# Eight table evacuations split by filter group, with a new order of the LN1 statistics and of the filter stages, in a one-core spectral block and gated FFN

## The chip, the cores and the metric

The kernel runs on one core of a Trainium2 chip. The metric is device time in microseconds (us) of one execution, as the median of several. All runs compared here are fast runs at full granted clock, except that three executions in two experiments (named below) show 0.997. A profile of one execution stands beside the times; its "span" runs from the first to the last instruction that it shows and is about 2 us shorter than the time. Engines: PE is the matmul engine, PEld its weight loads, DVE the vector, ACT the scalar engine, POOL the GpSimd. PSUM is the memory that the matmuls write, here used as eight banks; to evacuate a bank is to copy it into SBUF, the working memory, so that the bank can be written again.

## The reference, cut to what matters

```python
def _A_ref(x, w_r, w_i):                       # x: (1, 2048, 576)
    X = jnp.fft.rfft2(x.astype(jnp.float32), axes=(-2, -1))
    X = X * (w_r + 1j * w_i)
    return jnp.fft.irfft2(X, s=(S, D), axes=(-2, -1)).astype(jnp.bfloat16)
def _B_ref(x, w_gate, w_up, w_down):           # 576 -> 4608 -> 576
    return (_gelu(x @ w_gate) * (x @ w_up)) @ w_down
h  = x + _A_ref(_layernorm(x), A_w_r, A_w_i)
h2 = h + _B_ref(_layernorm(h), B_w_gate, B_w_up, B_w_down)
```

## The kernel before

The Fourier transforms are matmuls with constant tables, in this order:

- **Head.** x arrives in five transfers as 16 tiles. LN1, the first layer norm, takes each tile's variance, on DVE (`B`: two statistics instructions) or on ACT (`S` and `Q`: a sum and a sum of squares). Six groups of tiles follow: DVE aggregates (`v`), ACT takes the root (`q`), DVE the reciprocal (`c`), DVE or POOL scales the table (`x`), POOL negates half of x (`n`), PE multiplies (`M`), and five PSUM banks a group are evacuated to the tile `U` (`E0` to `E29`; `A` is ACT, `D` is DVE).
- **Filter stage.** For each of 16 frequency groups: `D` (six matmuls on U, evacuation CUS), `B` (four, evacuation YS), `T` and `Z` (products and sums with the spectral weights on DVE), `V` (four matmuls, evacuation), and five times `R` (two matmuls and an expansion VR on DVE).
- **Inverse, LN2, FFN.** Not changed.

An order of work is a list of words; each engine takes its own words in order, and the semaphores follow from the buffers named in `r` (read) and `w` (written).

```python
def a_bank(i, k):                    # the PSUM bank of evacuation (group i, part k)
    return (5 * i + AORD.index(k) + ABASE) % 8
def a_ev(n, eng):                    # one evacuation of the table stage
    ...
    dst = U[0:w, k, :, c0:c1, :].rearrange("p g n e -> p n g e")
    P.op(eng, fn, r=[("PS", b)], w=[("U", i, k)])
def st_D(i, eng=ACT):
    g = GORD[i]                      # 1 .. 15, 0
    ...   # each matmul reads all of U's part k
          r=uk[us] + ["FT"], w=[("PS", b)])
def st_T(i, ...):                    # DVE product of YS with the weights
    ...
```

Of the kernel before, what the change touches and what calls it, by code (L numbers as in the profile page):

```python
# [9 lines left out]
S, D, K2 = 2048, 576, 289  # L10
KW = 288
HK = 144
# [4 lines left out]
NG = 16  # L17
# [3 lines left out]
NPRE = 8  # L21
PARTS = ((0, 256), (256, 512))
GROUPS = ((0, 2), (2, 4), (4, 7), (7, 10), (10, 13), (13, 16))
SEQ1 = """k14 B0 B1 v0 Q2 S2 B3 q0 v1 n0 n2 c0 q1 S4 x0D c1 M0 E1A B6 E0A Q4 B5 B7 x1P v2 E2D n1 B8 E3A E4A k104 M1 q2 c2 B9 Q10 E5A E7A n3 v3 S10 B12 E6A q3 c3 x2P B11 k202 M2 E9A x3P Q13 v4 E12A E8A q4 n4 B14 c4 B15 E10A E11A S13 E13D M3 E14A E15A v5 x4P E16D q5 E17A c5 E18A M4 n5 x5D E20D E19A E22D E21A M5 E23D E24A E25A E27A E26D E29A E28D""".split()
LORD = "x0-2 x2-4 a0-4 x4-8 a4-8 x8-12 x12-16 a8-16".split()
ACT_TILES = tuple(int(w[1:]) for w in SEQ1 if w[0] == "Q")
SEQF = """w0 w1 D0 D1 D2 B0 T0 B1 T1 Z0 D3 B2 D4 B3 D5 T2 Z1 B4 Z2 D6 T3 T4 V0 D7 B5 Z3 B6 w2 Z4 R0 T5 V1 D8 Z5 B7 T6 Z6 D9 B8 T7 V2 D10 V3 Z7 T8 Z8 D11 B9 R1 V5 B10 w3 T10 T9 D12 Z10 V4 D13 B11 Z9 T11 V6 B12 Z11 B13 T12 D14 T13 V8 Z13 D15 V7 Z12 B14 R2 B15 T14 V10 T15b V9 Z14 V11 V13 T15a Z15a V12 V14 Z15b R3 V15 R4""".split()
VENG = [('act',), ('act',), ('act',), ('act',), ('act',), ('act',), ('act',), ('act',), ('act',), ('act',), ('act',), ('act',), ('act',), ('act',), ('act',), ('act', 'act')]
DENG, BENG = ['act', 'dve', 'dve', 'act', 'act', 'act', 'act', 'act', 'act', 'act', 'act', 'act', 'act', 'act', 'act', 'act'], ['dve', 'act', 'act', 'act', 'act', 'act', 'act', 'act', 'act', 'act', 'act', 'act', 'act', 'act', 'act', 'act']
QR = ((0, 2), (2, 3), (3, 4), (4, 8), (8, 16))  # L30
DSTEP, DLAG = (36, 22) if NPRE == 8 else (28, 22)
SEQ = """I0 I1 N0 I2 s0 N1 I3 s1 N2 I4 q0 s2 c0 N3 I5 s3 p1 q1 N4 q2 I6 N5 c1 c2 p0 A1 I7 n3 N6 A0 z3 N7 p2 D2 G0 G1""".split()
# [11 lines left out]
def build_tables():  # L44
# [8 lines left out]
    n1 = np.arange(128)[:, None]  # L53
    n2 = np.arange(16)[None, :]
    s = 16 * n1 + n2
    A = np.zeros((128, 16, 64, 2))
    I = np.zeros((64, 2, 16, 128))
    for j in range(64):
        if j == 0:
            A[:, :, 0, 0] = 1.0  # L60
            A[:, :, 0, 1] = (1 - 2 * (n1 % 2))
            I[0, 0] = 1.0
            I[0, 1] = (1 - 2 * (np.arange(128) % 2))[None, :]
        else:
            th = 2 * np.pi * ((j * s) % 2048) / 2048.0
            A[:, :, j, 0] = np.cos(th)
            A[:, :, j, 1] = -np.sin(th)
            I[j, 0] = np.cos(th).T
            I[j, 1] = -np.sin(th).T
    A = A.reshape(128, 16, 4, 16, 2).transpose(0, 1, 3, 2, 4)  # L70
    I = I.reshape(4, 16, 2, 16, 128).transpose(1, 0, 2, 3, 4)
    T["ATAB"] = A.reshape(128, 16 * 128)
    I = I.reshape(128, 16, 128)
# [19 lines left out]
    B = np.zeros((2, 3, 16, 4, 2, 128))  # L93
    V = np.zeros((2, 2, 128, 2, 16, 4, 2))
    nn = np.arange(16)
    for st in range(2):
        g = 1 - st
        for p in range(128):
            half, r, jj = p // 64, (p % 64) // 4, p % 4
            low = (g + 16 * jj) if half == 0 else _minus_rows(g)[jj]  # L100
            k = 128 * r + low
            w = np.exp(-2j * np.pi * ((k * nn) % 2048) / 2048.0)
            if low in (0, 64):
# [3 lines left out]
                c = np.conj(w)  # L107
# [5 lines left out]
            if half == 0:  # L113
                sl = jj
                e = np.exp(-2j * np.pi * ((r * nn) % 16) / 16.0)
                ca, cb = e, 1j * e
            else:
                sl = (128 - low - g) // 16
                rp = 15 - r
                e = np.exp(-2j * np.pi * ((rp * nn) % 16) / 16.0)  # L120
# [190 lines left out]
def _build(nc, A_x, A_w_r, A_w_i, B_w_gate, B_w_up, B_w_down, out):  # L311
    P = Prog(nc)
    T = build_tables()
    dram = {n: nc.inline_tensor(_np_bf16(T[n]), name="c_" + n.lower()) for n in T}
    PE, DVE, ACT, SP, POOL = "pe", "dve", "act", "sp", "pool"
# [50 lines left out]
    U = sb.alloc("U", [128, 5, NG, NT, 8], BF16)  # L366
# [7 lines left out]
    FT = sb.alloc("FT", [128, 6, 2 * HK], BF16)  # L374
# [26 lines left out]
    PS = nc.alloc_psum_tensor("PS", [128, 4096], F32)  # L401

    def bank(b, p0=0, p1=128, c0=0, c1=512):
        return PS[p0:p1, b * 512 + c0:b * 512 + c1]

    def banks(b, n, w):
        return PS[:, b * 512:(b + n) * 512].rearrange("p (a c) -> p a c", a=n)[:, :, 0:w]
# [17 lines left out]

    for i, w in enumerate(LORD):
        (x_load if w[0] == "x" else atb_load)(i, int(w[1:].split("-")[0]), int(w.split("-")[1]))
# [25 lines left out]
    GORD = list(range(1, NG)) + [0]  # L453
# [23 lines left out]
    def ln1_var(i):  # L477
        c0, c1 = GROUPS[i]
        for c in range(c0, c1):
            if c in ACT_TILES:  # L480
                P.op(DVE, lambda v, c=c: v.tensor_scalar(TM[:, 0, c:c + 1], SA[:, 0, c:c + 1], SA[:, 0, c:c + 1], 1.0 / (D * D), op0=ALU.mult, op1=ALU.mult), r=[("SA0", c)], w=[("TM", c)])
            else:
                P.op(DVE, lambda v, c=c: v.bn_aggr(MV1[:, c, :], ST1[:, c, :, :]), r=[("ST1", c, 0), ("ST1", c, 1)], w=[("MV1", c)])
        for c in range(c0, c1):
            if c in ACT_TILES:
                P.op(DVE, lambda v, c=c: v.tensor_scalar(MV1[:, c, 1:2], SA[:, 1, c:c + 1], 1.0 / D, TM[:, 0, c:c + 1], op0=ALU.mult, op1=ALU.subtract), r=[("SA1", c), ("TM", c)], w=[("MV1", c)])
# [23 lines left out]
    def a_bank(i, k):  # L510
        return (5 * i + AORD.index(k) + ABASE) % 8
# [19 lines left out]
                    P.op(PE, lambda t, b=b, lhs=lhs, p0=p0, p1=p1, s=s, e=e, o=o, c=c: t.matmul(bank(b, p0, p1, o, o + 128), lhs, ATS[:, c, :], start=s, stop=e),  # L531
                         r=[("X", c), ("ATS", c)] + ([("XN", c)] if k % 2 else []), w=[("PS", b)])

    def a_ev(n, eng):
        i, k = n // 5, AORD[n % 5]
        c0, c1 = GROUPS[i]
        n, b, w = c1 - c0, a_bank(i, k), 64 if k == 4 else 128
        src = bank(b, 0, w, 0, 128 * n).rearrange("p (n g e) -> p n g e", n=n, g=16)
        dst = U[0:w, k, :, c0:c1, :].rearrange("p g n e -> p n g e")
        fn = (lambda v: v.tensor_copy(dst, src)) if eng == DVE else (lambda a: a.activation(dst, src, ACTF.Copy))  # L540
        P.op(eng, fn, r=[("PS", b)], w=[("U", i, k)])

    def x_neg(i):
        c0, c1 = GROUPS[i]
# [1 line left out]
             r=[("X", c) for c in range(c0, c1)], w=[("XN", c) for c in range(c0, c1)])  # L546

    ENG = {"A": ACT, "D": DVE, "P": POOL}
    RUN1 = {"k": idle_mm, "S": act_sum, "Q": act_sq, "B": ln1_tile, "v": ln1_var, "q": ln1_sqrt, "c": ln1_rs, "M": a_mm, "x": ln1_scale, "E": a_ev, "n": x_neg}
    P.op(ACT, lambda a: a.activation(SA[:, 0, 0:1], EPT[:, 0:1], ACTF.Sqrt), r=["EPT"], w=[("SA0", 0)])  # L550
    for w in SEQ1:
        a = w[1:]
        RUN1[w[0]](*((int(a[:-1]), ENG[a[-1]]) if a[-1] in ENG else (int(a),)))


    c = 0
    while c < NT:
        c1 = c + 1
        while c not in ACT_TILES and c1 < NT and c1 not in ACT_TILES:
            c1 += 1  # L560
        src, f, keys = (SA[:, 0, c:c1], -1.0 / D, "SA0") if c in ACT_TILES else (MV1[:, c:c1, 0], -1.0, "MV1")
        P.op(POOL, lambda g, c=c, c1=c1, src=src, f=f: g.tensor_scalar(NM[:, c:c1], src, f, 1.0, op0=ALU.mult, op1=ALU.mult),
             r=[(keys, k) for k in range(c, c1)], w=[("NM", k) for k in range(c, c1)])
        c = c1
    P.alias([("XN", c) for c in range(NT)], [("V", g, c) for g in range(NG) for c in range(2)])
    uk = [[("U", i, k) for i in range(len(GROUPS))] + (["Uz"] if k == 4 else []) for k in range(5)]
    ukeys = [k for ks in uk for k in ks]
    LAST = NG - 1

    FB, used = {}, [0] * 8  # L570
    for t, w in enumerate(SEQF):
        k, i = w[0], w[1:].rstrip("abc")
        if k in "DB":
            late = ("V", 0) in FB or any(x[0] == "V" for x in SEQF[t:t + 4])
            b = min((0, 2, 4) if late else (0, 2, 4, 6), key=lambda b: max(used[b], used[b + 1]))
            used[b] = used[b + 1] = t + 1
        elif k in "VR":
            b = min((6, 7) if ("D", LAST) not in FB else range(8), key=lambda b: used[b])
            used[b] = t + 1
            if k == "V":  # L580
# [4 lines left out]
                b = (b, b2)  # L585
# [4 lines left out]
    def ev(eng, dst, src, r, w):  # L590
        fn = (lambda v: v.tensor_copy(dst, src)) if eng == DVE else (lambda a: a.activation(dst, src, ACTF.Copy))  # L591
        P.op(eng, fn, r=r, w=w)

    def st_D(i, eng=ACT):
        g = GORD[i]
        b0, s3 = FB["D", i], i % 3
        for o in range(2):
            b = b0 + o
            for m, us in enumerate((1 - o, 3 - o, 4) if o == 0 else (4, 1 - o, 3 - o)):
                P.op(PE, lambda t, b=b, m=m, us=us, o=o, g=g: t.matmul(bank(b, 0, 128, 0, 2 * HK), U[:, us, g, :, :], FT[:, 3 * o + (2 if us == 4 else us // 2), :], start=(m == 0), stop=(m == 2)),  # L600
                    r=uk[us] + ["FT"], w=[("PS", b)])
        ev(eng, CUS[:, s3, :, :].rearrange("p a (j r) -> p a j r", r=2), banks(b0, 2, 2 * HK).rearrange("p r (a j) -> p a j r", a=2),
           [("PS", b0), ("PS", b0 + 1)], [("CU", s3)])

# [59 lines left out]

    for w in SEQF:
        i = int(w[1:].rstrip("abc"))
# [42 lines left out]
    g0 = smm.index("G0")  # L709
    for t, w in enumerate(w for w in smm if w[0] != "G"):  # L710
        b = min((2, 3) if t >= g0 - 2 else range(4), key=lambda b: last[b])
# [251 lines left out]
def bass_sequential_preLN__spectral_gfnet__geglu_ffn__prompt_kernel(  # L963
    nc, A_x, A_w_r, A_w_i, B_x, B_w_gate, B_w_up, B_w_down, out
):
    _build(nc, A_x, A_w_r, A_w_i, B_w_gate, B_w_up, B_w_down, out)
# [28 lines left out]
```

## Time and profile before

| | before |
|---|---|
| median time | 492.23 us (3 runs, 492.04 to 492.62) |
| span of the profiled run | 490.0 us |
| PE busy | 484.2 us (99%) |
| x tiles 4 to 6 in hand (POOL starts on them) | 7.63 us |
| first d-transform matmul, D0 | 19.58 us |
| first B matmul, B0 | 21.95 us |
| first matmul of the inverse | 48.30 us |

PE is the critical engine, so the reader should look for the few places where it waits; those that the profile lists all lie before the inverse or at its start. The lines are in the prediction. The start times are those of the first instruction as the profile lists it; the chain of waits puts B0 at 22.12, 0.17 later, as it counts from the end of the matmul ahead.

### The profile page before, as it was taken

Reading aid. Unit: us, or ns where it says so; the run is one execution under the profiler, and the core shown is the slowest. Engines: PE = TensorE matmul, PEld = TensorE weight load, DVE = VectorE, ACT = ScalarE, POOL = GpSimd, SP = SyncE. Lnnn points to the kernel's source line nnn. Section 1 sums busy time; section 2 is a strip of 40 time slices with the busy share of each in tenths; the row PEclk is TensorE's granted clock in tenths of the full one; section 3 lists DMA queues with packets and bytes.
Section 4 is the critical chain, followed back from the end, with each engine's and each line's share of the span. In section 5 each row is a group of like instructions: output and inputs, shape, how many; then the busy total and the mean of one; then the engine's idle time right before and its main releaser. Section 6 shows DMA issues by size and latency. Waiting matters only on the chain.

```text
span 490.0 us, 9898 instructions
## 1 busy us (share of the span) xinstructions
PE 484.2 (99%) x4373; PEld 285.7 (58%) x4374; DVE 190.9 (39%) x381; ACT 150.9 (31%) x291; POOL 33.4 (7%) x61
## 2 busy tenths in 40 slices
PE   7999999999999999999999999999999999999998
PEld 3787754444588744444577644444677544444775
DVE  6999623443455534333311144433211233333111
ACT  6899852233222222322200033233100122323000
POOL 6411541000000020000000000000000000000000
PEclk9999999999999999999999999999999999999999
DMA  8990997211000071100000001000000000000000
GB/s 281 242 324 18 373 372 272 70 25 21 1 14 17 13 233 23 23 4 1 1 18 14 19 18 23 17 0 1 7 19 19 7 0 1 1 1 1 14 19 18
DMA packets 25147, 31.26 MB, mean 64 GB/s; under 512 B 11440, under 2 KB 17840, under 8 KB 25104
## 3 DMA queue, kind: packets, MB, share of 16 engines
q1 hardware_dynamic: 22208, 18.68, 13.1%
q0 software_dynamic: 2896, 11.95, 6.9%
q8 instruction: 34, 0.56, 0.5%
q14 instruction: 9, 0.07, 0.1%
HBM read 26.29 MB, written 2.36 MB: 58 GB/s over the span
## 4 chain that ended last, share of the span: by engine, by line
PE 96%; DVE 1%; DMA 1%; SPq 0%; POOL 0%; issue 0%; POOLq 0%; DVEq 0%
PE PS L839 57%; PE PS L926 29%; PE PS L600 2%; PE PS L610 2%; PE PS L531 1%; PE PS L717 1%; DMA XO<-in_A_x_dram 1%; PE PS L640 1%; PE PS L755 1%; PE PS L877 1%; DVE ST L475 1%; PE PS L891 0%; PE PS L804 0%; SPq L221 0%; DVE VR L655 0%; DVE TP L619 0%
## 5 line engine op out<-in xcount | busy, mean ns | idle before, releaser
L839 PE MATMUL PS<-HT,WG 64*128 64x512 bf16 (+1 forms) x2142 | 228.5, 373 | 0.0
L839 PEld LDWEIGHTS PS<-HT,WG 64*128 64x128 bf16 x2142 | 104.1, 94 | 122.7 <-issue 0.7
L848 DVE TENSOR_TENSOR AT<-GL,PS 128x512 bf16<-128x512 bf16 x144 | 99.0, 688 | 177.5 <-ACT GL L847 177.5
L847 ACT ACTIVATE GL<-PS 128x512 bf16<-128x512 f32 x144 | 85.9, 597 | 262.4 <-PE PS L839 248.9
L926 PE MATMUL PS<-WD,AT 128*128 128x288 bf16 (+2 forms) x1152 | 144.3, 286 | 0.0
L926 PEld LDWEIGHTS PS<-WD,AT 128*128 128x128 bf16 x1152 | 110.7, 98 | 30.8 <-ACT GL L847 1.3
L929 DVE TENSOR_TENSOR OS<-PS,XO 128x288 bf16<-128x288 f32 (+2 forms) x32 | 14.6, 458 | 100.4 <-PE PS L926 100.4
L839 PE MATMUL PS<-HT,WGX 64*128 64x512 bf16 x486 | 53.4, 376 | 0.0
L839 PEld LDWEIGHTS PS<-HT,WGX 64*128 64x128 bf16 x486 | 23.7, 94 | 28.7
L746 ACT ACTIVATE JD<-XO,NM 128x576 bf16<-128x576 bf16 x8 | 6.2, 776 | 28.4 <-DVE XO L894 28.4
L600 PE MATMUL PS<-FT,U 128*128 128x288 bf16 x96 | 14.2, 287 | 0.0
L619 DVE TENSOR_TENSOR TP<-YS,WS 128x1152 bf16<-128x1152 bf16 (+2 forms) x17 | 11.8, 718 | 0.3
L531 PE MATMUL PS<-ATS,XO 128*128 128x128 bf16 (+1 forms) x128 | 10.1, 221 | 1.4 <-POOL XN L545 0.8
L475 DVE BATCH_NORM_STATS2 ST<-XO 128x6 f32<-128x288 bf16 x24 | 9.3, 438 | 4.1 <-DMA XO<-in_A_x_dram 4.1
L600 PEld LDWEIGHTS PS<-FT,U 128*128 128x128 bf16 x96 | 9.2, 98 | 2.4 <-DVE U L540 0.2
L591 ACT ACTIVATE YS<-PS 128x576 bf16<-128x576 f32 x15 | 9.6, 651 | 2.0 <-PE PS L610 1.8
L531 PEld LDWEIGHTS PS<-ATS,XO 128*128 128x128 bf16 (+1 forms) x128 | 7.4, 97 | 4.4 <-POOL XN L545 1.3
L610 PE MATMUL PS<-CUS,BT 128*128 128x288 bf16 x64 | 10.0, 286 | 0.0
L591 ACT ACTIVATE CUS<-PS 128x576 bf16<-128x576 f32 x14 | 9.1, 650 | 0.8 <-PE PS L600 0.4
L894 DVE TENSOR_TENSOR XO<-PS,XO 128x576 bf16<-128x576 f32 x8 | 6.1, 758 | 8.0 <-PE PS L891 8.0
L640 PE MATMUL PS<-VT,ZS 128*128 128x256 bf16 x64 | 8.8, 273 | 0.3 <-DVE ZS L630 0.3
L591 ACT ACTIVATE V<-PS 128x512 bf16<-128x512 f32 (+1 forms) x17 | 9.0, 582 | 0.0
(79 smaller groups left out, 210.2 us busy)
## 6 DMA issues: line engine op xcount, KB each, us to landing
WD<-in_B_w_down_dram POOLq DMA_DIRECT2D x9, 576.0 KB, 10.7
WG<-in_B_w_up_dram SPq DMA_DIRECT2D x4, 1152.0 KB, 6.9
WG<-in_B_w_gate_dram POOLq DMA_DIRECT2D x4, 1152.0 KB, 9.7
out_dram<-OS SPq DMA_DIRECT2D x30, 72.0 KB, 1.6
XO<-in_A_x_dram SPq DMA_DIRECT2D x3, 576.0 KB, 7.0
WGX<-in_B_w_up_dram SPq DMA_DIRECT2D x1, 1152.0 KB, 6.0
WGX<-in_B_w_gate_dram POOLq DMA_DIRECT2D x1, 1152.0 KB, 9.9
HT<-HN SPq DMA_TRANSPOSE x60, 2.4
```

The costliest lines, as they stand in the source:

```text
L475: P.op(DVE, lambda v, c=c, h=h: v.bn_stats(ST1[:, c, h, :], XO[:, c, 288 * h:288 * h + 288]), r=[("X", c)], w=[("ST1", c, h)])
L531: P.op(PE, lambda t, b=b, lhs=lhs, p0=p0, p1=p1, s=s, e=e, o=o, c=c: t.matmul(bank(b, p0, p1, o, o + 128), lhs, ATS[:, c, :], start=s, sto ...
L591: fn = (lambda v: v.tensor_copy(dst, src)) if eng == DVE else (lambda a: a.activation(dst, src, ACTF.Copy))
L600: P.op(PE, lambda t, b=b, m=m, us=us, o=o, g=g: t.matmul(bank(b, 0, 128, 0, 2 * HK), U[:, us, g, :, :], FT[:, 3 * o + (2 if us == 4 else u ...
L610: P.op(PE, lambda t, b=b, tb=tb, m=m, s3=s3, sp_=sp_: t.matmul(bank(b, 0, 128, 0, KW), BT[:, sp_, tb, :], CUS[:, s3, m, :], start=(m == 0) ...
L619: P.op(DVE, lambda v: v.tensor_tensor(TP[:, sl, :, :, q0:q1], y4, w4, op=ALU.mult), r=[("Y", sl), ("Wn", i)] + (wkeys[0] if 1 <= g < 9 els ...
L640: P.op(PE, lambda t, b=b[c], c=c, zp=zp, sp_=sp_, z3=z3: t.matmul(bank(b, 0, 128, 256 * c, 256 * c + 256), ZS[:, z3, zp, c:256:2], VT[:, s ...
L839: op = P.op(PE, lambda t, h0=h0, kt=kt, wt=wt, b=b, s=(not second and j == 0), e=(second and j == n - 1): t.matmul(bank(b, 0, 128, c0, c1) ...
L847: P.op(ACT, lambda a: a.activation(GL[:, s2, :], bank(b0), ACTF.Gelu_apprx_tanh), r=[("PS", b0)], w=[("GL", s2)])
L848: P.op(DVE, lambda v: v.tensor_tensor(AT[:, f, :], GL[:, s2, :], bank(b0 + 1), op=ALU.mult), r=[("GL", s2), ("PS", b0 + 1)], w=[("AT", f)])
L926: P.op(PE, lambda t, b=b, d0=d0, d1=d1, f=f, p=p: t.matmul(bank(b, 0, 128, 0, d1 - d0), AT[:, f, 128 * p:128 * p + 128], WD[:, f, d0:d1], ...
L929: P.op(DVE, lambda v, b=b, d0=d0, d1=d1, p=p, c=c: v.tensor_tensor(OS[:, p % 2, d0:d1], bank(b, 0, 128, 0, d1 - d0), XO[:, c, d0:d1], op=A ...
```

## The change

The intent is to let the filter stage start before the last evacuations of the table stage are finished. The constant table is permuted so that filter group i reads slice i of U. Eight evacuations (22 to 29) are done in halves: slices 0 to 7, which D0 to D7 read, first; slices 8 to 15 later, under the first D stages. The LN1 order is new (three tiles on ACT in place of four, other evacuations on DVE), the filter order is new, and three evacuations (of D1, D2, B0) go from DVE to ACT.

```diff
-    A = A.reshape(128, 16, 4, 16, 2).transpose(0, 1, 3, 2, 4)
+    A = A.reshape(128, 16, 4, 16, 2).transpose(0, 1, 3, 2, 4)[:, :, list(range(1, NG)) + [0]]
-    def a_ev(n, eng):
+    def a_ev(n, eng, late=False):
+        hs = (1,) if late else (0,) if n in SPLIT else (0, 1)
+        g0, g1 = 8 * hs[0], 8 * hs[-1] + 8
...
-        P.op(eng, fn, r=[("PS", b)], w=[("U", i, k)])
+        P.op(eng, fn, r=[("PS", b)] + ([("EV", n)] if late else []),
+             w=[("U", i, k, h) for h in hs] + ([] if late else [("EV", n)]))
...
-                    r=uk[us] + ["FT"], w=[("PS", b)])
+                    r=[("U", q, us, i // 8) for q in range(len(GROUPS))] + ... + ["FT"], w=[("PS", b)])
...  # SEQ1 (cut): evacuations 7, 9 to 12 on ACT, and the end of the list; F is a late half
-  E5A E7A n3 v3 S10 B12 E6A q3 c3 x2P B11 k202 M2 E9A x3P Q13 v4 E12A E8A q4 ... E10A E11A S13 E13D M3
+  E5A E8A q3 k202 M2 B10 B12 E9A n4 E11A E12A S13 c3 B11 E10A E7A v4 x3P M3
-  M5 E23D E24A E25A E27A E26D E29A E28D
+  M5 E25A F23D F24A E26A F25D E27A E29A F29A E28D F28D F22A F26D F27A
...  # SEQF (cut): the tail
-  B14 R2 B15 T14 V10 T15b V9 Z14 V11 V13 T15a Z15a V12 V14 Z15b R3 V15 R4
+  B14 T13 Z12 D15 Z13 T14 V9 R2 V10 Z14 B15 V13 T15a T15b V11 Z15a V12 Z15b R3 V14 V15 R4
-DENG, BENG = ['act', 'dve', 'dve', 'act', ...], ['dve', 'act', ...]
+DENG, BENG = ['act', 'act', ...], ['act', ...]
```

More of the change, by code (lines that the diff above doesn't have):

```diff
@@ L23 @@
 GROUPS = ((0, 2), (2, 4), (4, 7), (7, 10), (10, 13), (13, 16))
-SEQ1 = """k14 B0 B1 v0 Q2 S2 B3 q0 v1 n0 n2 c0 q1 S4 x0D c1 M0 E1A B6 E0A Q4 B5 B7 x1P v2 E2D n1 B8 E3A E4A k104 M1 q2 c2 B9 Q10 E5A E7A n3 v3 S10 B12 E6A q3 c3 x2P B11 k202 M2 E9A x3P Q13 v4 E12A E8A q4 n4 B14 c4 B15 E10A E11A S13 E13D M3 E14A E15A v5 x4P E16D q5 E17A c5 E18A M4 n5 x5D E20D E19A E22D E21A M5 E23D E24A E25A E27A E26D E29A E28D""".split()
+SEQ1 = """k14 Q3 B1 B0 n0 S3 n2 v0 B2 v1 q0 q1 c0 x0D M0 S4 c1 Q4 B5 B6 E4A E2A v2 B7 q2 n1 E0A E1A x1P c2 k104 M1 B8 x2P B9 E6A n3 v3 E3A E5A E8A q3 k202 M2 B10 B12 E9A n4 E11A E12A S13 c3 B11 E10A E7A v4 x3P M3 B14 q4 c4 E13A E14A x4P B15 Q13 v5 E17A q5 E16A E15D M4 c5 E19A E20A x5D E18D E23A n5 E22D E21D E24A M5 E25A F23D F24A E26A F25D E27A E29A F29A E28D F28D F22A F26D F27A""".split()
 LORD = "x0-2 x2-4 a0-4 x4-8 a4-8 x8-12 x12-16 a8-16".split()
+SPLIT = tuple(int(w[1:-1]) for w in SEQ1 if w[0] == "F")
 ACT_TILES = tuple(int(w[1:]) for w in SEQ1 if w[0] == "Q")
-SEQF = """w0 w1 D0 D1 D2 B0 T0 B1 T1 Z0 D3 B2 D4 B3 D5 T2 Z1 B4 Z2 D6 T3 T4 V0 D7 B5 Z3 B6 w2 Z4 R0 T5 V1 D8 Z5 B7 T6 Z6 D9 B8 T7 V2 D10 V3 Z7 T8 Z8 D11 B9 R1 V5 B10 w3 T10 T9 D12 Z10 V4 D13 B11 Z9 T11 V6 B12 Z11 B13 T12 D14 T13 V8 Z13 D15 V7 Z12 B14 R2 B15 T14 V10 T15b V9 Z14 V11 V13 T15a Z15a V12 V14 Z15b R3 V15 R4""".split()
+SEQF = """w0 w1 D0 D1 D2 B0 T0 D3 B1 Z0 T1 B2 D4 T2 D5 Z1 B3 B4 T3 D6 Z2 w2 D7 Z3 B5 V1 V0 T4 T5 Z4 B6 w3 B7 T6 D8 Z5 T7 V2 D9 Z6 B8 T8 V3 Z7 V4 D10 B9 R0 D11 V5 Z8 B10 T9 R1 T10 B11 D12 Z9 V6 D13 Z10 B12 T11 D14 T12 B13 V8 Z11 V7 B14 T13 Z12 D15 Z13 T14 V9 R2 V10 Z14 B15 V13 T15a T15b V11 Z15a V12 Z15b R3 V14 V15 R4""".split()
 VENG = [('act',), ('act',), ('act',), ('act',), ('act',), ('act',), ('act',), ('act',), ('act',), ('act',), ('act',), ('act',), ('act',), ('act',), ('act',), ('act', 'act')]
-DENG, BENG = ['act', 'dve', 'dve', 'act', 'act', 'act', 'act', 'act', 'act', 'act', 'act', 'act', 'act', 'act', 'act', 'act'], ['dve', 'act', 'act', 'act', 'act', 'act', 'act', 'act', 'act', 'act', 'act', 'act', 'act', 'act', 'act', 'act']
+DENG, BENG = ['act', 'act', 'act', 'act', 'act', 'act', 'act', 'act', 'act', 'act', 'act', 'act', 'act', 'act', 'act', 'act'], ['act', 'act', 'act', 'act', 'act', 'act', 'act', 'act', 'act', 'act', 'act', 'act', 'act', 'act', 'act', 'act']
 QR = ((0, 2), (2, 3), (3, 4), (4, 8), (8, 16))
@@ L532, in a_mm @@
                          r=[("X", c), ("ATS", c)] + ([("XN", c)] if k % 2 else []), w=[("PS", b)])
-    def a_ev(n, eng):
+    def a_ev(n, eng, late=False):
         i, k = n // 5, AORD[n % 5]
+        hs = (1,) if late else (0,) if n in SPLIT else (0, 1)
+        g0, g1 = 8 * hs[0], 8 * hs[-1] + 8
         c0, c1 = GROUPS[i]
-        n, b, w = c1 - c0, a_bank(i, k), 64 if k == 4 else 128
-        src = bank(b, 0, w, 0, 128 * n).rearrange("p (n g e) -> p n g e", n=n, g=16)
-        dst = U[0:w, k, :, c0:c1, :].rearrange("p g n e -> p n g e")
+        m, b, w = c1 - c0, a_bank(i, k), 64 if k == 4 else 128
+        src = bank(b, 0, w, 0, 128 * m).rearrange("p (n g e) -> p n g e", n=m, g=16)[:, :, g0:g1, :]
+        dst = U[0:w, k, g0:g1, c0:c1, :].rearrange("p g n e -> p n g e")
         fn = (lambda v: v.tensor_copy(dst, src)) if eng == DVE else (lambda a: a.activation(dst, src, ACTF.Copy))
-        P.op(eng, fn, r=[("PS", b)], w=[("U", i, k)])
+        P.op(eng, fn, r=[("PS", b)] + ([("EV", n)] if late else []), w=[("U", i, k, h) for h in hs] + ([] if late else [("EV", n)]))
     def x_neg(i):
@@ L548, in _build @@
     ENG = {"A": ACT, "D": DVE, "P": POOL}
-    RUN1 = {"k": idle_mm, "S": act_sum, "Q": act_sq, "B": ln1_tile, "v": ln1_var, "q": ln1_sqrt, "c": ln1_rs, "M": a_mm, "x": ln1_scale, "E": a_ev, "n": x_neg}
+    RUN1 = {"k": idle_mm, "S": act_sum, "Q": act_sq, "B": ln1_tile, "v": ln1_var, "q": ln1_sqrt, "c": ln1_rs, "M": a_mm, "x": ln1_scale, "E": a_ev, "F": lambda n, eng: a_ev(n, eng, True), "n": x_neg}
     P.op(ACT, lambda a: a.activation(SA[:, 0, 0:1], EPT[:, 0:1], ACTF.Sqrt), r=["EPT"], w=[("SA0", 0)])
@@ L565, in _build @@
     P.alias([("XN", c) for c in range(NT)], [("V", g, c) for g in range(NG) for c in range(2)])
-    uk = [[("U", i, k) for i in range(len(GROUPS))] + (["Uz"] if k == 4 else []) for k in range(5)]
+    uk = [[("U", i, k, h) for i in range(len(GROUPS)) for h in range(2)] + (["Uz"] if k == 4 else []) for k in range(5)]
     ukeys = [k for ks in uk for k in ks]
@@ L594, in st_D @@
     def st_D(i, eng=ACT):
-        g = GORD[i]
         b0, s3 = FB["D", i], i % 3
@@ L599, in st_D @@
             for m, us in enumerate((1 - o, 3 - o, 4) if o == 0 else (4, 1 - o, 3 - o)):
-                P.op(PE, lambda t, b=b, m=m, us=us, o=o, g=g: t.matmul(bank(b, 0, 128, 0, 2 * HK), U[:, us, g, :, :], FT[:, 3 * o + (2 if us == 4 else us // 2), :], start=(m == 0), stop=(m == 2)),
-                    r=uk[us] + ["FT"], w=[("PS", b)])
+                P.op(PE, lambda t, b=b, m=m, us=us, o=o: t.matmul(bank(b, 0, 128, 0, 2 * HK), U[:, us, i, :, :], FT[:, 3 * o + (2 if us == 4 else us // 2), :], start=(m == 0), stop=(m == 2)),
+                    r=[("U", q, us, i // 8) for q in range(len(GROUPS))] + (["Uz"] if us == 4 else []) + ["FT"], w=[("PS", b)])
         ev(eng, CUS[:, s3, :, :].rearrange("p a (j r) -> p a j r", r=2), banks(b0, 2, 2 * HK).rearrange("p r (a j) -> p a j r", a=2),
```

## The prediction

> **What bounds the kernel now.** I read the page's busy shares first, then the stages, then the chain of work that ended last, then each engine's instructions in order of time between 3 and 50 us. The page:
>
> ```profile
> PE 484.2 (99%) x4373; PEld 285.7 (58%) x4374; DVE 190.9 (39%) x381; ACT 150.9 (31%) x291; POOL 33.4 (7%) x61
> PE 96%; DVE 1%; DMA 1%; SPq 0%; POOL 0%; issue 0%; POOLq 0%; DVEq 0%
> ```
>
> The first line is busy time, the second the shares of the chain: TensorE (PE) carries it. The change takes no matmul away, so it can only win time in which PE waits. Everything after the spectral part (from 59.9 us) is left alone and is PE back to back. The stages before it:
>
> ```profile
> 10.00:15.00 5.00, 4.35 (x65) 3.32 (x66) 5.00 (x25) 4.80 (x18) 3.44 (x5) 1.00 1.06 340
> 15.00:20.00 5.00, 4.99 (x83) 4.13 (x82) 4.96 (x18) 4.87 (x15) 3.59 (x12) 1.00 1.10 245
> 40.00:50.00 10.00, 9.46 (x81) 7.37 (x79) 8.81 (x20) 8.76 (x19) 2.63 (x4) 1.00 0.21 55
> ```
>
> Columns: stretch, length, then busy us of PE, PE's weight loads, DVE, ACT, POOL, then clock, DMA share, GB/s. In 10 to 20 us (LN1 statistics, table matmuls, their evacuations) DVE and ACT are full; PE is fed by them. In 40 to 50 us PE loses half a microsecond. The chain of waits says where:
>
> ```profile
> 11.54 0.83 POOL ATS L500
> 12.38 0.05 issue
> 12.42 3.69 PE PS L531 x60
> 16.12 0.01 issue
> 16.13 3.61 PE PS L531 x60
> 19.74 2.37 PE PS L600 x18
> 22.12 0.98 PE PS L610 x8
> ...
> 44.10 1.32 PE PS L640 x12
> 45.42 0.04 issue
> 45.46 0.22 DVE TP L619
> ...
> 47.29 0.88 DVE VR L655
> 48.17 0.14 issue
> 48.30 1.63 PE PS L717 x12
> ```
>
> Start, us, what. From 12.42 us PE is the chain but for two places. First, 18 d-transform matmuls take 2.37 us where 18 x 0.122 = 2.20 would do: 0.17 us lost. PE's weight loads say to whom:
>
> ```profile
> 20.22 1.58 PEld L600 LDWEIGHTS PS<-FT,U 128*128 128x128 bf16 x14 [0.23 <-DVE U L540]
> ```
>
> D0 had been started, with four weights, before this and then waited for the last evacuation of the table stage: the very wait the change aims at. Second, from 45.42 to 48.30 the chain runs over DVE products and sums and the R expansion (VR).
>
> **What the Trainium skill says.** "Perfetto Trace Analysis", Optimizing Scalar/DVE Operations: breaking up instructions may let work complete sooner where Scalar/Vector cause bubbles on other engines without being saturated. Here they are saturated at that moment (windows above), so the split must pay its own fixed cost. "ScalarE: Activation LUTs", What ACT_TABLE_LOAD costs: an ACTIVATE is 186 ns plus 0.833 ns a column, and neighbours overlap by about 93 ns. This trace has 372 ns for 256 columns and 502 for 384, 1.02 ns a column, steeper than the page; the eight evacuations from 16.91 us take 3.37 us, 0.41 apart, so the overlap of 0.09 agrees. "PSUM — Partial Sum Buffer", PSUM bank collisions: two engines must not be in one bank and quadrant at once, reads included. That is why the late half waits for the early half's key; no run here shows a collision.
>
> **The change, part by part.**
>
> (1) Eight evacuations (numbers 22 to 29) in halves of 192 columns, storage groups 0 to 7 first; D0 to D7 need only the first halves. The table's groups are permuted in the host-made constant, free on the chip. A 192-column ACT half is an estimate of 372 - 64 x 1.02 = 307 ns, about 0.22 apart, so two halves cost 0.44 against 0.41; on DVE (0.54 for 384, 0.405 for 256, about 0.47 apart) halves are about 0.34 long and 0.27 apart. Extra engine time is near 8 x 0.05 = 0.4 us over two engines, but some 1.8 us leave the path before D0. After the last table matmul ACT needs one half (about 0.1 + 0.31 us), and D0 first reads that tile 0.37 + 0.12 us after its start. So the 0.17 us go. The later halves also free PSUM banks: D1 needs bank 3 (late half 26, last on DVE), D2 bank 4 (late half 27, last on ACT). They end about 0.7 and 1.1 us after D0's start; needed at 1.1 and 1.5. Tight, but no wait.
>
> (2) LN1 order. Removed from DVE before the last scaling (x5): two of the three evacuations there (0.33 + 0.54 us) and one pair of the ACT-statistics merges; added: one statistics tile (0.71). Walking DVE's new order from 7.58 us with the spacings of the trace (tile 0.73, aggregate group 0.25, with a merge 0.42, reciprocal 0.08, evacuation 0.47, x5 0.5): reciprocals c2 at 10.3 (before 11.25), c3 13.45 (12.97), c4 15.2 (14.88), x5 ends 17.5 to 17.9 (17.86). POOL's scaling takes 0.83 us plus 0.13 to start. So table group M2 can start at x2's end, 11.4, or after M1 (10.05 + 1.11) and two fillers (0.43), that is 11.6 instead of 12.42. But M3 needs x3 (13.62 + 0.13 + 0.83 = 14.6) and bank 0, freed by evacuation 7, which now stands on ACT behind three evacuations, the sum pass of tile 13 and evacuation 10: sqrt at 12.14, then 0.2 + 0.27 + 0.41 + 0.41 + 0.69 + 0.41 = 14.5, plus 0.36 = 14.9. So M3 starts near 14.9, not 14.17. Groups M3, M4, M5 take 30 x 0.0557 = 1.67 us each: D0 near 19.7 if only x3 and x4 (16.33) bind, 19.95 if evacuation 7 does; before 19.58. What M2 gains, M3 gives back.
>
> (3) The three evacuations of D1, D2 and B0 go from DVE to ACT: DVE loses 0.75 x 3 = 2.2 us, ACT gains 3 x 0.55. ACT then has 32 x 0.55 + 8 for V = 25.6 us to do in about 27, DVE drops to some 23 to 25. D0's CU evacuation starts near 21.05, behind late half 27, and CU0 is out by 21.7; B0 starts at D0's start + 3 x 0.733 = 21.9 to 22.15. No wait there. So B0 starts in 21.9 to 22.15 against 22.12 in the chain: a gain of 0 to 0.2.
>
> (4) New filter order. PE's work from B0 to the inverse is fixed: 78 D x 0.122 + 64 B x 0.122 + 64 V x 0.109 + 10 R x 0.109 = 25.4 us. Before: 22.12 + 25.4 = 47.55, but the inverse began at 48.30, so about 0.75 was lost, nearly all in the tail. In the new tail B15 stands two V stages later, followed by V13, V11, V12, R3, V14 (4 x 0.437 + 0.22 = 1.97 us). From B15's end the path to V15 is 0.1 + 0.65 (YS on ACT) + 0.6 (T15a and T15b to Z's start) + 0.15 + 0.42 (Z15a) + 0.1, about 2.0 to 2.1: a stall near 0.1 in place of 0.31. Then V15's first half must leave PSUM (0.38 + 0.1) while R4 gives PE 0.22 of work. R3's output is no longer in bank 0, which the inverse's first matmul writes, but in bank 2, its third. I put the loss at 0.4 instead of 0.75: gain 0.3 to 0.4.
>
> Sum of the expected path: head about 0.1, tail 0.35, together 0.4 to 0.5 us of 492.2.
>
> **The rivals.** (a) The wait moves: evacuation 7 holds M3, or a late half holds bank 3 or 4, so D0 comes 0.4 later and eats the gain. For it: ACT and DVE are full (4.9 of 5 us) in that stretch. Time 492.2 to 492.5. (b) ACT becomes the bound of the filter stage: 25.6 of 27 us leaves little for waits in order; V and CU evacuations queue and PE stalls in the middle. Against it: the new order puts more PE work between dependent stages, and before the change ACT had only 1.65 us less. Time up to 493. (c) The DMAs set the head: x lands at 3.66, 4.36, 7.56 and 10.2 us and no load order changes, so M0, M1 and what needs tile 8 cannot move. This holds in any case and caps the gain of the head near 0.5. (d) Everything falls well, x3 binds M3, the tail has no stall: 0.8 us, 491.4.
>
> **Range and chances.** 492.23 - 0.45 = 491.8. The three runs of before span 0.6 us, and the rivals span 491.3 to 492.6, so 8 in 10 for 491.2 to 492.4. Two per cent is 9.8 us; all idle time of PE before 59.9 us is under 7 us and no matmul is added, so neither side of 2% is plausible: 0.01 each.
>
> **What would show it.** Step 1: no PE weight-load wait on U in D0, and the first 18 D matmuls in 2.20 us. Step 2: M2 starts near 11.6, then PE idles over 1 us before M3 at 14.6 to 14.9, its releaser an ACT evacuation; D0 at 19.7 to 19.95. Step 3: no PE wait on CU near 22 us; ACT busy 90% or more from 21 to 46 us. Step 4: the inverse starts near 47.8 instead of 48.30. The rest of the span, from the inverse to the end, keeps its 441.7 us (490.0 - 48.30). It would be wrong if PE stalls on ACT in mid filter stage, if M3 comes later than 15.2, or if the later inverse or gate stage changes length by more than 0.2.

## The result

The changed kernel takes 492.11 us (median of 6 runs, 491.85 to 492.36); the kernel before took 492.13 us in its 6 runs. The ratio is 0.9998, with a 95% interval of 0.9985 to 1.0011: the same. Ratios and intervals here are formed from the fast runs of the same rounds, so they are not quite the ratio of the medians quoted.

The page of the changed kernel has these busy times, against those that the prediction showed for before:

```profile
PE 484.1 (99%) x4374; PEld 285.7 (58%) x4374; DVE 188.7 (38%) x380; ACT 152.7 (31%) x297; POOL 33.1 (7%) x58
```

DVE has lost 2.2 us of work and ACT has gained 1.8, as meant, and PE has what it had. The stretches (columns as in the prediction) show where PE has less to do and where more:

```profile
10.00:15.00 5.00, 3.54 (x52) 2.72 (x53) 5.00 (x21) 4.49 (x15) 3.67 (x5) 1.00 1.09 312
15.00:20.00 5.00, 5.00 (x87) 4.37 (x88) 4.46 (x18) 4.89 (x16) 2.92 (x8) 1.00 1.08 221
40.00:50.00 10.00, 9.70 (x82) 7.57 (x80) 9.30 (x24) 8.89 (x19) 2.44 (x4) 1.00 0.15 32
```

From 10 to 15 us PE is busy 3.54 us where it was 4.35: a hole of 0.8 us more. PE's instructions in order of time (start, length, what, and in brackets the idle time before it with its releaser) name it. The line numbers have moved by one to two: L532 is the table matmul, L602 the D, L612 the B, L642 the V and L719 the inverse.

```profile
15.00 0.23 PE L532 MATMUL PS<-ATS,XO 128*128 128x128 bf16 x1 [1.20 <-ACT U L543]
...
20.17 2.37 PE L602 MATMUL PS<-FT,U 128*128 128x288 bf16 x18
22.38 0.29 PE L612 MATMUL PS<-CUS,BT 128*128 128x288 bf16 x1
```

Table group M3 starts at 15.00 us, after 1.20 us of idle PE, released by an evacuation on ACT. Then D0 follows at 20.17 and B0 at 22.38. ACT's own order shows which evacuation that is:

```profile
12.34 1.30 ACT L543 ACTIVATE U<-PS 128x256 bf16<-128x256 f32 x3
13.54 0.67 ACT L467 ACTIVATE JNK<-XO 128x576 bf16<-128x576 bf16 x1
14.12 0.19 ACT L467 ACTIVATION_READ_ACCUMULATOR JNK<-XO 128x1 f32 x1
14.21 0.74 ACT L543 ACTIVATE U<-PS 128x384 bf16<-128x384 f32 x2
```

The last line is evacuations 10 and 7; it ends at 14.95, and evacuation 7 frees bank 0, into which M3 writes first. POOL had scaled M3's table from 13.72 to 14.55 us, so PE could have gone 0.4 us sooner. The split itself works: the weight loads of D0 to D2 run through, with no wait on U.

```profile
20.12 2.11 PEld L602 LDWEIGHTS PS<-FT,U 128*128 128x128 bf16 x18
```

The starts cut the span into parts that can be compared one by one. The first, up to x tiles 4 to 6 in hand, is a transfer that varies from run to run (7.58 to 8.23 us in the profiles); the others are the same to 0.02 us wherever the order of work is the same.

| us | before | changed | difference |
|---|---|---|---|
| x tiles 4 to 6 in hand | 7.63 | 7.70 | chance |
| from there to D0 (head) | 11.95 | 12.47 | +0.52 |
| D0 to B0 | 2.37 | 2.21 | -0.16 |
| B0 to the inverse (filter stage) | 26.35 | 26.24 | -0.11 |
| the inverse to the end of the span | 441.7 | 441.7 | 0 |

The parts that the change can set sum to +0.25 us. Over the timed runs the median span rises too, from 490.1 (nine runs beside the first experiments) to 490.3. That the time does not rise is owed to what lies outside the span: 492.12 - 490.1 = 2.02 us before, 1.74 to 1.85 in the six runs of the changed kernel. No profile shows what that part is.

### The profile page after: what moved, and what is told of

The parts are those of the page before. It is cut to its first block, busy times and chain, and to the rows that moved or that the text cites. A ratio compares the mean times of both kernels' runs of the same rounds, so it can differ in the third digit from the quotient of the medians.

```text
span 490.3 us, 9902 instructions
## 1 busy us (share of the span) xinstructions
PE 484.1 (99%) x4374; PEld 285.7 (58%) x4374; DVE 188.7 (38%) x380; ACT 152.7 (31%) x297; POOL 33.1 (7%) x58
## 3 DMA queue, kind: packets, MB, share of 16 engines
q0 software_dynamic: 2896, 11.95, 7.0%
HBM read 26.29 MB, written 2.36 MB: 58 GB/s over the span
## 4 chain that ended last, share of the span: by engine, by line
PE 95%; DVE 2%; DMA 1%; issue 1%; POOL 0%; ACT 0%; SPq 0%; DVEq 0%; POOLq 0%
PE PS L841 57%; PE PS L928 29%; PE PS L602 2%; PE PS L532 2%; PE PS L719 1%; DMA XO<-in_A_x_dram 1%; PE PS L612 1%; PE PS L757 1%; PE PS L879 1%; DVE TP L621 1%; PE PS L642 1%; DVE VR L657 0%; DVE ZS L632 0%; PE PS L893 0%; POOL XN L548 0%
## 5 line engine op out<-in xcount | busy, mean ns | idle before, releaser
L602 PE MATMUL PS<-FT,U 128*128 128x288 bf16 x96 | 13.7, 286 | 0.0
L532 PE MATMUL PS<-ATS,XO 128*128 128x128 bf16 (+1 forms) x128 | 10.1, 221 | 2.1 <-ACT U L543 1.2
L602 PEld LDWEIGHTS PS<-FT,U 128*128 128x128 bf16 x96 | 9.3, 98 | 2.3
L594 ACT ACTIVATE CUS<-PS 128x576 bf16<-128x576 f32 x16 | 10.4, 655 | 0.5 <-PE PS L602 0.2
L532 PEld LDWEIGHTS PS<-ATS,XO 128*128 128x128 bf16 (+1 forms) x128 | 7.5, 97 | 4.7 <-ACT U L543 1.4
L543 ACT ACTIVATE U<-PS 128x256 bf16<-128x256 f32 (+5 forms) x29 | 9.7, 391 | 1.0 <-PE PS L532 0.8
L612 PE MATMUL PS<-CUS,BT 128*128 128x288 bf16 x64 | 10.0, 286 | 0.0
L642 PE MATMUL PS<-VT,ZS 128*128 128x256 bf16 x64 | 8.8, 273 | 0.2 <-DVE ZS L632 0.2
```

Source lines behind the costliest of these rows:

```text
L532: P.op(PE, lambda t, b=b, lhs=lhs, p0=p0, p1=p1, s=s, e=e, o=o, c=c: t.matmul(bank(b, p0, p1, o, o + 128), lhs, ATS[:, c, :], start=s, sto ...
L594: fn = (lambda v: v.tensor_copy(dst, src)) if eng == DVE else (lambda a: a.activation(dst, src, ACTF.Copy))
L602: P.op(PE, lambda t, b=b, m=m, us=us, o=o: t.matmul(bank(b, 0, 128, 0, 2 * HK), U[:, us, i, :, :], FT[:, 3 * o + (2 if us == 4 else us // ...
L612: P.op(PE, lambda t, b=b, tb=tb, m=m, s3=s3, sp_=sp_: t.matmul(bank(b, 0, 128, 0, KW), BT[:, sp_, tb, :], CUS[:, s3, m, :], start=(m == 0) ...
L642: P.op(PE, lambda t, b=b[c], c=c, zp=zp, sp_=sp_, z3=z3: t.matmul(bank(b, 0, 128, 256 * c, 256 * c + 256), ZS[:, z3, zp, c:256:2], VT[:, s ...
```

## The experiments

Twelve runs were made of eleven kernels (e13 is e8 once more), each with four to six timed executions beside the kernel before. Since a few tenths are at stake and the intervals of the times are about 0.13% (0.6 us) to each side, the verdicts rest on the parts of the span from the traces; the times are given beside them.

**e1: evacuation 7 earlier.** Theory: what the change won was lost by M3's wait for bank 0. Rival: something else came late too.

```diff
-  M2 B10 B12 E9A n4 ... B11 E10A E7A v4
+  M2 B10 B12 E7A E9A n4 ... B11 E10A v4
```

> The changed kernel with evacuation 7 moved on ACT from behind evacuation 10 to ahead of evacuation 9. Theory A (what the change won before D0 was given back by table group M3 waiting 1.20 us for bank 0): M3 starts at the end of its scaling, near 14.6 us instead of 15.00, D0 near 19.8 instead of 20.17, and the inverse and the end come 0.3 to 0.4 us earlier. Theory B (M3 is held by something else that came late too, or the later stage absorbs it): D0 or the inverse does not move by more than 0.1 us.

Measured: 491.95 us, ratio 0.9997 (0.9984 to 1.0009). The head takes 12.15 us instead of 12.47, the other parts 2.20 and 26.24 as in the changed kernel. In this run x was in hand only at 7.94, so the absolute starts (M3 14.93, D0 20.09) moved less than was expected; from the landing, M3 starts 6.99 us later, not 7.30. PE's line says what holds M3 now:

```profile
14.93 0.22 PE L532 MATMUL PS<-ATS,XO 128*128 128x128 bf16 x1 [0.89 <-POOL ATS L501]
```

Both are partly right. Bank 0 cost 0.32 us of the 0.52. Now M3 waits for its scaling on POOL; the reciprocal ahead of that stands behind two statistics tiles on DVE (`v3 B10 B12 c3`) where it stood behind one (`v3 B12 c3`), and comes 0.38 us later from the landing (13.66 - 7.94 against 12.97 - 7.63). The other 0.20 goes with this later scaling, as far as the trace shows; no run tests it alone.

**e2: no split.** All evacuations whole again, all else kept.

```diff
-  M5 E25A F23D F24A E26A F25D E27A E29A F29A E28D F28D F22A F26D F27A
+  M5 E25A E26A E27A E29A E28D
```

> The changed kernel with all evacuations whole again (late halves taken out), all else kept. Theory A (the split is worth the wait of D0 on the last evacuations, about 0.2 us): the weight loads of D0 wait again 0.2 to 0.4 us, the 18 first d matmuls take 2.4 us or more, and B0 and the inverse come 0.2 us later than in the changed kernel. Theory B (the split costs as much engine time as it saves): D0's wait returns but B0's evacuation and the inverse are at the same place within 0.1 us.

Measured: 492.19 us, ratio 1.0002 (0.9989 to 1.0014). D0 to B0 takes 2.36 us instead of 2.21, head 12.47 and filter stage 26.24 as in the changed kernel. The wait in D0 is back:

```profile
20.84 1.46 PEld L602 LDWEIGHTS PS<-FT,U 128*128 128x128 bf16 x13 [0.17 <-ACT U L543]
```

So the split is worth 0.15 us here, and its extra instructions cost nothing that shows.

**e3: the split alone.** The kernel before with the late halves added; LN1 order, filter order and engines as before.

```diff
-  M5 E23D E24A E25A E27A E26D E29A E28D
+  M5 E23D E24A F24A F23D E25A E27A F25A E26D E29A E28D F27A F26D F28D F29A F22D
```

> The kernel before with the split alone (LN1 order, filter order and engines of before). Theory A: D0 at 19.6 us, no wait on U, first 18 d matmuls in 2.20 us, inverse near 48.1 instead of 48.30, total about 0.15 us under the kernel before. Theory B: late halves hold D1 or D2 or the three evacuations on DVE, and B0 comes no earlier than 22.1.

Measured: 491.91 us, ratio 0.9996 (0.9983 to 1.0010). Head 11.95, D0 to B0 2.21, filter stage 26.36. The split gives its 0.16 us in the other surroundings too, and no late half holds a bank.

**e4: the filter order and engines of before**, in the changed kernel.

```diff
 # SEQF, DENG and BENG as in the kernel before
```

> The changed kernel with the filter order and evacuation engines of before (split and new LN1 order kept). Theory C (the new filter order gains nothing, since DVE's products and sums from T0 to T15 bound that stage in both orders): from B0's start to the inverse 26.2 us as in both, inverse at 48.6 to 48.8. Theory D (the new order wins 0.3 us in the tail that another cost hides): inverse at 48.9 or later.

Measured: 492.22 us, ratio 1.0003 (0.9990 to 1.0015). Head 12.48, D0 to B0 2.20, filter stage 26.35. The inverse started at 48.99, but x was in hand only at 7.96, so the parts decide: the new filter order is worth 0.11 us, not 0 and not 0.3. That its reason is DVE's load, as theory C said, is tested next.

**e5: two negations from DVE to POOL.** `w2` and `w3` negate weights for filter groups 8 to 15; POOL does no arithmetic of its own there and only issues transfers.

```diff
-            P.op(DVE, lambda v, g0=g0, g1=g1: v.tensor_scalar(WS[:, 0, g0:g1, :], ...
+            P.op(POOL if i > 1 else DVE, lambda v, g0=g0, g1=g1: v.tensor_scalar(WS[:, 0, g0:g1, :], ...
```

> The changed kernel with the negations w2 and w3 (1.1 us of DVE work in the filter stage) moved to POOL, which is idle there. From the landing of x tiles 4 to 7 to D0 12.47 us and from D0 to B0 2.21 us, as in the changed kernel. Theory E (DVE's backlog sets when T15 and Z15 are done, so it sets the tail): from B0 to the inverse 25.9 to 26.0 us instead of 26.24. Theory F (DVE is only as busy as PE lets it be, and the tail is latency): still 26.2. Theory G (POOL and DVE disturb each other): longer than 26.3, with T products longer than 0.75 us.

Measured: 494.57 us, ratio 1.0061 (1.0048 to 1.0075); the profiled execution at full clock took 494.38, while two of the six ran at a clock of 0.997 and 496.0 to 496.1 (without these two the median is 494.45). The filter stage takes 28.51 us. Theory G holds. The first line is POOL's, from POOL's list in order of time:

```profile
24.79 3.32 POOL L626 TENSOR_SCALAR WS<-WS 128x1156 bf16<-128x1156 bf16 x1 [5.75 <-DMA WS<-in_A_w_i_dram]
```

The next are DVE's of the same time:

```profile
25.01 2.89 DVE L635 TENSOR_TENSOR ZR<-TP 128x64 bf16<-128x64 bf16 x1
27.82 0.75 DVE L621 TENSOR_TENSOR TP<-YS,WS 128x1152 bf16<-128x1152 bf16 x1
```

The negation takes 3.32 us on POOL where DVE needs 0.46, and a DVE sum of 64 columns that takes 0.18 us elsewhere stands 2.89 us, until POOL is about done; the second T product after it, beside the second negation, takes 1.45 us instead of 0.75. The Trainium skill's page "SBUF — State Buffer", sections SBUF: two separate sides and Who interferes with whom, says that a DVE instruction with two SBUF inputs contends with a GpSimd instruction that reads SBUF, and that whoever starts first blocks the other for its whole instruction. For the first negation this trace agrees: POOL began 0.22 us ahead, and the sum has two SBUF inputs. For the second (28.26 to 30.83 us) it does not agree on the whole instruction: a sum of 512 columns, again with two SBUF inputs, takes its usual 0.41 us from 29.87, in the midst of it. Either the block ends earlier or POOL's listed span is too long; the trace does not tell. Nor is 3.32 us POOL's pace elsewhere: in the head it negates 864 columns in 0.91 us, and why it is slower here is not shown. The experiment therefore says nothing on DVE's load.

**e6: D1, D2 and B0 on DVE again**, in the changed kernel.

```diff
-DENG, BENG = ['act', 'act', ...], ['act', ...]
+DENG, BENG = ['act', 'dve', 'dve', 'act', ...], ['dve', 'act', ...]
```

> The changed kernel with D1, D2 and B0 evacuated on DVE again, as before the change. Theory E (DVE sat idle 2.06 us waiting for the first YS, so taking the three evacuations away freed nothing that could be used): D0 to B0 2.2 us and B0 to the inverse 26.2 us, both within 0.1 of the changed kernel. Theory H (ACT, full at 98%, is what bounds the filter stage): the inverse 0.3 us or more earlier. Theory I (the move was worth its 2.2 us on DVE in part): the inverse 0.2 us or more later.

Measured: 492.72 us, ratio 1.0012 (0.9998 to 1.0025). In the trace the head takes 12.47, D0 to B0 2.21, the filter stage 26.24: the same as in the changed kernel in every part. So in the traced parts the move of three evacuations is worth nothing. DVE cannot use the time it gains, as this line of the changed kernel shows: its first product waits 2.06 us for the first YS.

```profile
23.86 0.76 DVE L621 TENSOR_TENSOR TP<-YS,WS 128x1152 bf16<-128x1152 bf16 x1 [2.06 <-ACT YS L594]
```

The four timed runs have spans of 490.2 to 490.8 and 2.09 to 2.16 us outside the span. The profile is of the fastest of them, and the 0.3 to 0.6 us by which the others' spans exceed it have no trace; whether the move is worth something there stays open.

**e8: the LN1 order of before** with the split, the new filter order and the new engines. This is e3 with SEQF, DENG and BENG of the changed kernel.

```diff
 # SEQ1 as in e3; SEQF, DENG and BENG as in the changed kernel
```

> Split, new filter order and engines kept, but the LN1 order of before. If the parts simply add: landing to D0 11.95, D0 to B0 2.21, B0 to the inverse 26.24, sum 40.40 against 40.67 before and 40.92 with the whole change, so 0.25 us under the kernel before in the trace. If they do not add (the new filter order needs the new LN1 order): B0 to the inverse 26.35 or more.

Measured: 491.67 us, ratio 0.9993 (0.9979 to 1.0006). Head 11.94, D0 to B0 2.21, filter stage 26.24, sum 40.39 us. The parts add. x was in hand only at 8.16 us in the profiled execution, which fits its time (492.06), the slowest of the four; the other three have no trace.

**e10: e8 with the negations on POOL.**

```diff
 # e8 with the edit of e5
```

> Split, new filter order, LN1 order of before, and w2 and w3 on POOL. By theory E 40.40 less 0.3, 40.1 from the landing to the inverse, 0.55 us under the kernel before, near 491.6 us in the timed runs; by theory F 40.4 and 491.85.

Measured: 493.89 us, ratio 1.0041 (1.0027 to 1.0055; one run at a clock of 0.997). Filter stage 28.52 us. It fails for e5's reason and repeats it.

**e11: no negations, a wrong result** (relative error 0.03): `w2` and `w3` are left out, and filter groups 8 to 15 read a plane that exists.

```diff
+        if i > 1:
+            return
-    ... [NG * K2, 2], [-NG * K2, 2], [1, q1 - q0]])
+    ... [NG * K2, 2], [-NG * K2 if i < 8 else 0, 2], [1, q1 - q0]])
```

> The changed kernel without the negations w2 and w3, 1.1 us of DVE work; the products of filter groups 8 to 15 then read the wrong plane, so the result is wrong on purpose, at the same instruction sizes. Theory E: DVE ahead by up to 1.1 us, B0 to the inverse 25.9 to 26.0 us. Theory F (in mid stage DVE waits for YS from ACT and ACT for PE, so freed DVE time turns into waiting and only the last stretch counts): 26.2 within 0.1.

Measured: 492.25 us, ratio 1.0003 (0.9990 to 1.0016). Filter stage 26.24 us, to the hundredth. The list of waits (engine, line, awaited; us in total, times, longest) of the changed kernel's DVE from 22 us to the inverse has

```profile
DVE TP L621 <- ACT YS L594: 2.6, 2, 2.1
```

and that of this experiment

```profile
DVE TP L621 <- ACT YS L594: 3.3, 4, 2.1
```

So 1.1 us less work on DVE becomes 0.7 us more of counted waiting for YS. DVE's total does not bound the stage; theory E falls.

**e9: R2 earlier.** The 1.2 us expansion VR2 stands on DVE between T14 and T15 in the new tail. R2 is moved ahead of B14, in e8.

```diff
-  V8 Z11 V7 B14 T13 Z12 D15 Z13 T14 V9 R2 V10
+  V8 Z11 V7 R2 B14 T13 Z12 D15 Z13 T14 V9 V10
```

> The kernel of the LN1 order of before with split and new filter order, and the stage R2 moved up from between T14 and Z14 to ahead of B14 (no instruction more or less). Theory J (in the new tail the 1.2 us expansion VR2 stands on DVE right in front of Z14 and T15, and that is what keeps V15 late): V15 and the inverse come 0.3 us earlier, B0 to the inverse 25.9 to 26.0 us. Theory E (DVE's total is what counts, wherever VR2 stands): 26.24 within 0.05, or longer.

Measured: 492.60 us, ratio 1.0011 (0.9997 to 1.0024). Filter stage 27.15 us, 0.9 longer. The new place got another PSUM bank from the allocator, the one that V8 had filled just before:

```profile
43.01 0.28 PE L654 MATMUL PS<-VT,ZR 128*128 128x256 bf16 x1 [0.42 <-ACT V L594]
```

and DVE, next in its order, sat idle for 0.89 us in front of VR2. The move brought its own wait and so does not settle theory J.

**e12: VR2 short, wrong** (within the reference's tolerance): 256 of its 1024 columns; the rest are zeros written at the start.

```diff
+    P.op(POOL, lambda g: g.memset(VR[:, :, :, 9:13, :], 0.0), w=[("V", g_, 2) for g_ in range(9, 13)])
+        n = 1 if q == 2 else n
```

> The changed kernel with the expansion VR2 cut from 1024 to 256 columns (1.22 to about 0.42 us), its other three groups filled with zeros by POOL at the start: wrong on purpose. Theory J (VR2, standing between T14 and T15, is what keeps V15 late): T15 starts when its YS is out, 0.3 us sooner, V15 comes 0.2 to 0.3 us sooner, B0 to the inverse 25.9 to 26.05 us. Theory K (the end of YS15 or V's evacuations on ACT bind as closely): 26.15 to 26.24.

Measured: 492.16 us, ratio 0.9999 (0.9987 to 1.0012). VR2 takes 0.41 us. T15 now waits for YS15 instead of VR2 (0.46 us idle on DVE), and V15 starts 25.03 us after B0 instead of 25.28. Its wait for the sum Z15a is shorter but not gone, as the weight loads of V15 show, first in the changed kernel and then in this run:

```profile
47.66 0.33 PEld L642 LDWEIGHTS PS<-VT,ZS 128*128 128x128 bf16 x4 [0.46 <-DVE ZS L632]
47.69 0.33 PEld L643 LDWEIGHTS PS<-VT,ZS 128*128 128x128 bf16 x4 [0.32 <-DVE ZS L633]
```

Yet the filter stage takes 26.14 us, only 0.10 less and at the edge of theory K's range, because the inverse now waits for ACT:

```profile
48.81 0.28 PE L721 MATMUL PS<-DT,V 128*128 128x288 bf16 x1 [0.29 <-ACT V L595]
```

ACT evacuates six V pieces in a row there, 46.33 to 48.95 us. So two limits lie 0.1 us apart in the tail: DVE's run of products, sums and VR2, and ACT's queue of V evacuations behind YS15. Theory J holds for V15 (0.25 us sooner), theory K for the inverse.

**e13: e8 once more.**

> The kernel with the LN1 order of before, the split and the new filter order once more, unchanged, to see whether its 491.67 us repeats: 491.6 to 491.95 if the parts add (0.25 us under the kernel before in the trace), 492.1 or more if that was chance.

Measured: 491.71 us, ratio 0.9990 (0.9976 to 1.0003). Head 11.95, D0 to B0 2.20, filter stage 26.24; x in hand at 7.62 us, span 489.7. Against e8's profile x came 0.54 us sooner and the span is 0.5 shorter, with equal parts after it: the scatter between runs of one kernel is, in these two, the landing of x. The two runs of this kernel are the lowest medians, 0.43 and 0.53 us under the kernel before in the same rounds and about 0.4 under the changed one, which ran in other rounds. Against the kernel before, 40.67 - 40.39 = 0.28 us of this is in the traced parts and some 0.2 is outside the span (1.74 to 1.86 us here, 2.02 before). Each interval alone still holds 1.0. This kernel, the change without its LN1 order, beats both by what the traces and the medians say.

## Why the prediction was right or wrong

The time, 492.11 us, is in the range of 491.2 to 492.4, and "within 2%" is right. The point, 491.8, assumed a gain of 0.45 us that did not come. By its steps:

1. **The split.** Right. D0's wait went, the 18 D matmuls ran without a gap, and the late halves held no bank: -0.16 us, where 0.17 was said (e2 and e3 show it both ways).
2. **The LN1 order.** The mechanism was right and named: M2 sooner, M3 held by evacuation 7 at 14.9 us (15.00 measured) with more than 1 us of idle PE before it. What failed is the size of its sum, "So B0 starts in 21.9 to 22.15 against 22.12 in the chain: a gain of 0 to 0.2". B0 came at 22.54 in the chain, 0.39 after the late end of that. Of this, 0.22 is D0, put "at 19.7 to 19.95" and measured at 20.17: a table group took 5.17 / 3 = 1.72 us, not 1.67, and M3 came 0.1 later than said, 0.07 of it with x. The other 0.17 is a slip of bases: 19.95 + 2.2 is a start as the list gives it, where before is 21.95, but it was held against the chain's 22.12. On one base the prediction's own figures were no gain, but from 0.05 us sooner to 0.20 later. Of the head's +0.52, 0.32 is bank 0 (e1); the other 0.20 goes with the later scaling of M3, which no run tests alone.
3. **Three evacuations from DVE to ACT.** Right that no wait follows; e6 shows that they were worth nothing in the trace, and that DVE idles before T0 explains it. The prediction claimed no gain from them.
4. **The new filter order.** The step that failed: "I put the loss at 0.4 instead of 0.75: gain 0.3 to 0.4". Measured -0.11 (changed against before, and e4). The 0.75 has the same slip: 22.12 is a start of the chain, and from B0's 21.95 in the list 26.35 - 25.4 = 0.95 was lost before, and 0.84 after. With 0.109 us for each V and R matmul, as in the prediction, PE now loses 0.13 us before R3 (gone in e12), 0.34 before V15 and 0.29 before the inverse, where the prediction had 0, 0.1 and 0.26; before the change it lost 0.47 before V15 and 0.39 before the inverse. So what failed is the wait of V15, with that of R3. The path from B15 to V15 left out VR2, which the new order puts in front of Z14 and T15. The chain of waits of the changed kernel has it:

```profile
44.29 0.67 DVE TP L621
44.95 1.13 DVE VR L657
46.09 0.33 DVE ZS L632
...
46.52 0.75 DVE TP L621 x2
...
47.66 0.61 PE PS L642 x4
...
48.62 0.41 PE PS L719 x2
```

T15 starts at 46.52 in this chain though YS15 was out at 46.14 on ACT (started 45.49, 0.65 long). And even with VR2 cut to a third of its time the gain is 0.21 (26.35 - 26.14, e12) and not 0.35: V15 still waits, now for the end of YS15, and the term "0.38 + 0.1" for V15's evacuation left out the V pieces queued ahead of it on ACT.
5. **What was not in the prediction:** 0.2 us less outside the span. In the sum it hides the 0.25 us that the traced parts lost, so that the time lies nearer to the point than the reasoning would have it: this is luck. With 2.02 us outside, the median span of 490.3 would have made 492.3, still in the range. Nothing here tells its cause.

Of the rivals, (a), a moved wait, is what happened, with evacuation 7. (b) did not happen: the trace puts no wait of PE in the filter stage down to ACT, and the first loss found is the 0.13 us before R3; ACT comes up as a limit only in e12, at the very end of the stage. (d) did not happen: M3 waited for bank 0 and V15 for Z15a, and behind that wait e12 shows the second limit. The rest of the span kept its 441.7 us, as said.

## What to carry to other kernels

Before a split or a reorder is built, write down for each buffer who must free it and where that instruction now stands in its engine's order: the split's 0.16 us was paid for twice over, 0.32 us, by one evacuation moved behind others. Where a tail is set by a chain over two engines, count everything in each engine's queue between the first and the last link, and look for the second engine's limit close behind the first; here it was 0.1 us behind. And cut the span at a few fixed events, so that tenths of a microsecond can be added up part by part when the times themselves scatter by as much.

## What the Trainium skill lacked or had wrong

- "ScalarE: Activation LUTs" gives 0.833 ns a column plus 186 ns, and these runs do not show it wrong: the 1.02 ns a column in the prediction comes from two shapes of the kernel before (372 ns for 256 columns, 502 for 384), while in the changed kernel the same shapes took 377 and 479, 0.80 a column, and the 128-partition halves of 192 columns 331, where an estimate from the page's figures is 346. What the page lacks is a word on why evacuations of one shape differ so with the order around them.
- "SBUF — State Buffer" says that the loser is blocked for the whole instruction. In e5 the first negation on POOL did so (a DVE sum of 0.18 us took 2.89), but within the second, 2.57 us long, a DVE sum of the same kind ran in its usual 0.41 us.
- No page that I read has it that the time outside the traced span differs between kernels that differ in little but the order of the instructions: 2.02 us for the kernel before, 1.74 to 1.85 for the changed one, 2.09 to 2.16 for e6, 1.74 to 1.82 for e4, which has the evacuation engines of e6.
